# Sinkhorn block attention and token mixer on one core: attention ordered by head pairs, the first batch's V turned on TensorE

## Chip, cores and metric

The kernel runs on one NeuronCore of a Trainium2 chip. The metric is device time in microseconds (us) of one execution: median 109.06 us over three runs of the kernel before (108.4 to 109.84). The profiled execution took 109.01 us, of which the profile's span covers 107.0 us. In what follows a time "at 24.9 us" is counted from the start of that span.

## The reference

```python
for _ in range(5):                                   # sort_net: (4, 8, 8, 8), "Sinkhorn"
    P = np.exp(P - np.max(P, axis=-1, keepdims=True))
    P = P / (np.sum(P, axis=-1, keepdims=True) + 1e-09)
    P = P / (np.sum(P, axis=-2, keepdims=True) + 1e-09)
k_sorted = einsum('bhij,bhjcd->bhicd', P, k_b)       # k, v, q: (4, 8, 768, 64), as 8 blocks of 96
v_sorted = einsum('bhij,bhjcd->bhicd', P, v_b)
scores = scale * q_b @ k_sorted_b^T                  # within each block: 96 x 96
attn = softmax(scores); y = attn @ v_sorted_b
x = y as (4, 768, 512)                               # heads side by side
wq = x @ w_q ; wk = x @ w_k                          # 512 -> 64
mixed = (scale * wq @ wk^T) @ x                      # a token mixer, computed as wq @ (wk^T @ x)
out = relu(mixed) @ w_out                            # (4, 768, 512) fp32
```

## The kernel before

The four batches pass through one pipeline. All inputs are loaded from HBM by DMAs that GpSimd issues, which turn fp32 into bf16: per batch one load of Q, one of K, one of V (786,432 bytes each in SBUF), with three buffers for each of the three, so that the loads of batch 3 reuse the buffers of batch 0. Tokens are laid out so that a partition holds six consecutive tokens (`r` = 0..5) of each head.

The order of the whole program is written out by hand. `ORDER` is a string of items such as `K112`: a letter, a batch, a number and a last character, which for TensorE work is a PSUM bank and for the others an engine (A is ScalarE, D VectorE, P GpSimd, S SyncE). The program walks through it, so each engine gets its instructions in this order and takes them strictly in turn. A capital letter is work on TensorE, and the small letter of the same kind is the copy that takes the result out of PSUM:

- `l`: a load (number 0 is Q, 1 is K, 2 is V, 3 and 4 the weights `wqk` and `wo`). `c`: one of the five Sinkhorn steps (0 subtracts the first maximum), an exponential on ScalarE (L157) and six small VectorE operations. `i`: constants (`idb` the identity, `Lx` a selector, `m_p` a mask, ones and zeros in buffers).
- `U`, `b`, `B`: `U` turns the Sinkhorn result `Pb` on TensorE, `b` copies it to `PbT`, and `B` spreads it over the partitions with eight matmuls by `Lx`. `n`: the product of that with the mask gives `M`, the sorting weights of a batch (L218), for four heads at a time; batch 0 and 1 in parts on VectorE straight from PSUM, the others on GpSimd from the copy `PTR` (`u`).
- `Q`/`q`: 16 transposes each, three per batch, give `QT`. `K`/`k`: 12 matmuls each for a pair of heads (number 0 to 3), sort K and turn it at once, giving `KT`. `V`/`v`: 8 matmuls each, three per batch, give the sorted V in `Vs` with a column of ones beside each head (stride 65).
- `R`: six DMAs per batch on SyncE's queue turn `Vs` (tokens over 128 partitions) into `VT` (96 tokens of a block over 96 partitions).
- `S`/`e`: scores of five (block, head pair) cases each, seven per batch, and their exponential into `E` (L301). `P`, `r`, `x`: weighted sums with 14 (block, head) cases each, five per batch; the ones column yields the softmax's denominator, `r` takes its reciprocal and `x` multiplies (L333), giving `X`.
- `T`/`t`: transposes of `X` into `XT`; `J`/`j`: both 512-to-64 products; `d`, `W`/`w`: moving and turning them; `G`/`g`: wk^T x; `H`/`h`: times wq, with relu, into `mixT`; `O`/`o`: six products with `w_out` of four 512-column matmuls each; `y`: the stores.
- `Z`: matmuls on a buffer of zeros (`fil`) whose result nobody reads. `N`: a one-element GpSimd copy (`gate`) that makes GpSimd wait for an eviction before it goes on to the next loads in its order.

Two details decide when things can start. Scores are numbered by block first (`i, kp = divmod(pr, NP)`, L292), so every group of scores needs the sorted K of all four head pairs. And in `ORDER` K of batch 0 is the fourth load, behind Q and V of batch 0 and K of batch 1; the last three are V of batch 3, K of batch 3 and V of batch 2.

All matmuls are recorded at line 138, all plain copies at L142 (ScalarE) and L144 (VectorE).

Of the kernel before, what the change touches and what calls it, by code (L numbers as in the profile page):

```python
# [18 lines left out]
l00P l02P l11P i00P i03P i02P l01P c00D Z087 c01D i01D c02D l10P Z027 c03D Z027 c04D Q026 Q007 q02A  # L19
c05D Z025 q00A U004 Z026 b00D B007 Z026 n00D u00A Z025 n10P n01D Q014 Z025 q01A V000 n11P Z025 v00D  # L20
K112 K104 k11A V016 k10D R00S Z021 R01S v01A V022 K120 v02D N00v N01v N02v l12P l21P l03P K134 R02S
k12A R03S K036 k13A R04S K010 R05S K022 k03A k01D K004 k02A n20P k00D Z027 l04P Z027 n21P S030 S062
S054 e03A S006 e00A S010 e05A Q127 Q116 e01A q12D S024 q11D Q107 e06A l20P e02A S040 q10D Z026 e04A
Z025 S102 S154 P030 e10A P016 r03D e15A V102 x03D l30P v10A S144 r01D P040 x01D e14A P022 R11S R10S
r04D P006 r02D x04D S114 x02D T031 e11A r00D t03A K202 x00D T020 k20A K234 t02D T011 k23D T007 t01A
V112 J010 t00A S134 v11A j01D S166 J001 d01D e13A W010 R12S V122 j00D R13S w01D e16A n30P W001 v12D
N10v N11v N12v l32P l31P l22P K224 w00A S126 k22A G001 d00D n31P R15S K212 e12A R14S G011 k21D g01A
Q200 H004 q20A H012 Q211 h00D Q227 h01A q21D H024 q22A O010 h02D S252 o01A S206 O051 e25A S214 e20A
o05D S222 O020 e22A P106 e21A O001 r10D x10D o02A P112 P134 o00D S236 Q310 r11D y00S e23A r13D x11D
O031 q31A x13D V326 T103 v32A O040 o03D t10D P144 y01S o04A S246 r14D S262 Q301 x14D e24A y02S Q320  # L30
q30D K314 e26A T137 q32D k31A K322 t13D K300 k32D K334 k30A P126 k33A V312 r12D R34S V300 x12D R35S
v31A S324 v30D e32A S356 R32S T113 R33S T122 e35A t11D S304 R31S S310 t12D R30S J103 e30A V206 e31A
j10D J112 v20D d10S V224 j11A W103 V210 v22A d11S w10D W112 R20S S366 v21D G103 R21S w11A R25S e36A
S334 R24S G113 e33A R23S S340 R22S g11D P346 e34A H122 r34D H114 x34D h12A H100 h11D P326 h10A O143
r32D x32D P224 o14A O122 r22D x22D P200 o12A P216 r20D P242 x20D O135 O114 r21D o13A r24D x21D P230
y11S o11A O105 x24D r23D T214 x23D o10A T207 P312 t21A y10S P305 t20D T231 r31D r30D T220 x31D t23A
J204 O157 t22D j20A x30D J214 o15A T313 d20D j21A y12S T302 t31D W205 d21S W214 t30A P330 w20D G203
w21A r33D J302 x33D G213 j30A T327 g21A W302 d30A T336 t32D w30A H210 t33D H204 H222 h21D G307 h20A
J316 h22A O205 j31D O224 d31A o20D W316 O215 o22D w31A G317 o21A O234 g31A y20S H320 o23A H312 H306
O245 h31A y21S h30D O254 o24A O307 o25A h32D O335 y22S o30D O354 o33D y33S O327 y36S o35A O315 y38S  # L40
o32A O344 y35S o31D y34S o34A y37S
# [4 lines left out]
def kernel(  # L46
# [11 lines left out]
    nc = tc.nc  # L58
# [8 lines left out]
    D1 = D + 1  # L67
    DM = moe_w_out.shape[0]
# [36 lines left out]
    Vs = tiles("Vs", 2, [P, R6, H, D1])  # L105
    VT = tiles("VT", 2, [BLK, NB, H * D1])
    E = tiles("E", 2, [BLK, NT, EW])
    X = tiles("X", 2, [BLK, NB, DM])
# [12 lines left out]
    PbT = sb.tile([NB * NB, BH], BF16, name="PbT")  # L121
    Lx = sb.tile([NB * NB, NB, NB, SP], BF16, name="Lx")
# [4 lines left out]
    fil = sb.tile([P, 512], BF16, name="fil")  # L127

# [21 lines left out]
    def u_c(b, n, e):  # L150
        if n == 0:
            nc.vector.memset(Pm[:, NB:NB + 1, :], 1e-9)
            nc.vector.memset(fil, 0.0)  # L153
            nc.vector.reduce_max(tmp, Pv, axis=AX.X)
            nc.vector.tensor_sub(Pv, Pv, rows(tmp))
            return
        nc.scalar.activation(Pv, Pv, ACT.Exp)  # L157
        nc.vector.reduce_sum(tmp, Pv, axis=AX.X)
        nc.vector.reciprocal(tmp, tmp)
        nc.vector.tensor_mul(Pv, Pv, rows(tmp))  # L160
        nc.vector.reduce_sum(tmp, Pm.rearrange("p i j -> p j i"), axis=AX.X)
        nc.vector.reciprocal(tmp, tmp)
        nc.vector.tensor_mul(Pb if n == 5 else Pv, Pv, cols(tmp))


    def u_i(b, n, e):
        if n == 0:
            nc.gpsimd.memset(idb, 0.0)
            nc.gpsimd.affine_select(out=idb, in_=idb, compare_op=ALU.not_equal, fill=1.0, base=0,
                                    pattern=[[-1, P]], channel_multiplier=1)  # L170
        elif n == 1:
            nc.vector.reduce_max(m_p, idb.rearrange("p (j s) -> p s j", s=SP), axis=AX.X)
        elif n == 3:
            nc.gpsimd.memset(Lx, 0.0)
            nc.gpsimd.affine_select(out=Lx.rearrange("p i j s -> p (i j) s"),
                                    in_=Lx.rearrange("p i j s -> p (i j) s"),
                                    compare_op=ALU.not_equal, fill=1.0, base=0,
                                    pattern=[[-1, NB * NB], [0, SP]], channel_multiplier=1)
        elif n == 2:
            for t in Vs:  # L180
                nc.gpsimd.memset(t[:, :, :, D:D1], 1.0)
            for t in KT:
                nc.gpsimd.memset(t[:, :, S:S + P - BLK], 0.0)
            for t in E:
                nc.gpsimd.memset(t[:, :, 2 * TH * BLK:EW], 0.0)
                nc.gpsimd.memset(t[:, NT - 1, 2 * (NB * NP - TH * (NT - 1)) * BLK:EW], 0.0)
# [12 lines left out]
    def u_U(b, n, bank):  # L199
        mm(bf(bank)[0:NB * NB, 0:BH], Pb.rearrange("p i j -> p (i j)"), idb[0:BH, 0:BH], t=True)  # L200

    def u_b(b, n, e):
        nc.vector.tensor_copy(PbT, bf(U["t"])[0:NB * NB, 0:BH])

    def u_B(b, n, bank):
        for i in range(NB):
            mm(PS[:, bank, i * BH:(i + 1) * BH], Lx[:, i].rearrange("p j s -> p (j s)"), PbT)
# [3 lines left out]
    def u_n(b, n, e):  # L211
        h0, h1 = n * 4, n * 4 + 4
        if b == 0:
            src = PS[:, U["bank"], 0:NB * BH].rearrange("p (i h) -> p h i", h=BH)
        else:
            src = PTR.rearrange("p i h -> p h i")
        src = src[:, b * H + h0:b * H + h1, :]
        ENG[e].tensor_tensor(  # L218
            out=M[b % 2][:, h0:h1], in0=src.unsqueeze(2).to_broadcast([P, 4, SP, NB]),
            in1=m_p.unsqueeze(1).unsqueeze(3).to_broadcast([P, 4, SP, NB]), op=ALU.mult)  # L220
# [5 lines left out]
    def u_Z(b, n, bank):  # L226
        for _ in range(n):
            mm(PS[:, bank, :], fil[:, 0:P], fil)
# [10 lines left out]
    def u_q(b, n, e, bank):  # L239
        copy(e, QT[b % 2][:, :, 2 * n:2 * n + 2, :].rearrange("p k r s -> p k (r s)"),  # L240
             bf(bank).rearrange("p (k s) -> p k s", k=NP))

# [26 lines left out]

    def u_R(b, n, e):  # L270
        ENG[e].dma_start(out=VT[b % 2].rearrange("(s r) i x -> r s i x", r=R6)[n],
                         in_=Vs[b % 2][:, n].rearrange("p h e -> p (h e)"))


    def u_N(b, n, e):
# [7 lines left out]
        elif e == "e":  # L283
            src = t[0:1, n, 0:1]
        else:
            src = t.rearrange("p i m -> p (i m)")[0:1, grp(n)[0] * D:grp(n)[0] * D + 1]
# [3 lines left out]
    def u_S(b, n, bank):  # L290
        for m, pr in enumerate(range(n * TH, min(n * TH + TH, NB * NP))):
            i, kp = divmod(pr, NP)  # L292
# [18 lines left out]
    def u_P(b, n, bank):  # L311
        u0, w = grp(n)
        for m in range(2 * w):
# [3 lines left out]
            mm(PS[:, bank + a, c * D1:(c + 1) * D1], E[b % 2][:, t, x * BLK:x * BLK + P],  # L317
               VT[b % 2][:, u // H, (u % H) * D1:(u % H + 1) * D1])

    def avps(bank, w):  # L320
        return PS[0:BLK, bank:bank + 2, 0:w * D1].rearrange("p a (t e) -> p a t e", e=D1)
# [8 lines left out]
    def u_x(b, n, e, bank):  # L330
        u0, w = grp(n)
        xo = X[b % 2].rearrange("p i m -> p (i m)")[:, u0 * D:(u0 + 2 * w) * D]
# [5 lines left out]
    def u_T(b, n, bank):  # L338
        ps = bf(bank).rearrange("p (t c) -> p t c", t=PT)
        for ii in range(2):  # L340
            for pt in range(PT):
                mm(ps[:, pt, ii * BLK:(ii + 1) * BLK], X[b % 2][:, 2 * n + ii, pt * P:(pt + 1) * P],
                   idb[0:BLK, 0:BLK], t=True)

    def u_t(b, n, e, bank):
        copy(e, XT[b % 2][:, :, 2 * n:2 * n + 2, :].rearrange("p t i c -> p t (i c)"),
             bf(bank).rearrange("p (t c) -> p t c", t=PT)[:, :, 0:2 * BLK])

    def u_J(b, n, bank):
        for pt in range(PT):  # L350
            mm(PS[:, bank, 0:S // 2], wqk[:, pt].rearrange("p a d -> p (a d)"),
               XT[b % 2][:, pt, 4 * n:4 * n + 4, :].rearrange("p i c -> p (i c)"),
# [22 lines left out]
    def u_G(b, n, bank):  # L375
        for i in range(4 * n, 4 * n + 4):
            for a in range(2):
                mm(PS[a * DH:(a + 1) * DH, bank, 0:DM // 2], wk[b % 2][:, i, :],
                   X[b % 2][:, i, a * 256:(a + 1) * 256], start=(i == 0), stop=(i == NB - 1))
# [50 lines left out]
    fills = dict(q="Q", k="K", v="V", e="S", r="P", x="P", t="T", j="J", w="W", g="G", h="H", o="O")  # L430
    for item in ORDER.split():
        kind, b, n, arg = item[0], int(item[1]), int(item[2:-1]), item[-1]
        if kind.isupper() and kind not in "RN":
            banks[kind, b, n] = int(arg)
            if kind in "UB":
                U["t" if kind == "U" else "bank"] = int(arg)
# [36 lines left out]
```

The softmax here doesn't subtract the row's maximum and nothing guards it: scores larger than these inputs give would overflow.

## Time and profile before

| | busy us | share of the 107.0 us |
|---|---|---|
| TensorE matmuls (PE) | 91.9 | 86% |
| VectorE (DVE) | 70.7 | 66% |
| ScalarE (ACT) | 69.8 | 65% |
| GpSimd (POOL) | 27.4 | 26% |
| the queue of the loads | - | 62.7% of 16 DMA engines |
| SyncE's queue (`R`, `y`) | - | 27.5% of 16 DMA engines |

The busy time of a pipelined matmul includes its latency, so it overstates TensorE; of the 91.9 us, 11.9 us are the 30 matmuls on zeros. The text of the prediction reads it from the spacing of matmuls instead.

### The profile page before, as it was taken

The numbers are of one execution on the slowest core, as the hardware profiler recorded it, in microseconds if no ns is written. First come the engines' busy times: TensorE is split into PE (matmuls) and PEld (weight loads), VectorE is DVE, ScalarE is ACT, GpSimd is POOL, SyncE is SP. The second block draws the span as 40 slices with busy tenths as digits, with TensorE's granted clock in tenths as the row PEclk, the third lists the DMA queues.
The fourth block names the chain that finished last, engine by engine and source line by source line (L and its number), as shares of the span: only waits on it lengthen the run. The fifth ranks groups of instructions, "written<-read, shape, count | busy, mean of one in ns | idle before, by whom it ended". The sixth has DMA issues, their size and how long they took to land.

```text
span 107.0 us, 3324 instructions
## 1 busy us (share of the span) xinstructions
PE 91.9 (86%) x1407; PEld 60.9 (57%) x1419; DVE 70.7 (66%) x131; ACT 69.8 (65%) x99; POOL 27.4 (26%) x43
## 2 busy tenths in 40 slices
PE   5917689987798799999999987997999999999930
PEld 2306036774766677755768974864677865534400
DVE  1787550773429968693699994878999768528320
ACT  4104413686999689989689896895266758474420
POOL 6999226049980004880000000000000000000000
PEclk9995555999999999999999999999999999999999
DMA  0899999999999999999999999473045320045981
GB/s 3 91 203 204 203 204 204 204 239 224 222 201 193 202 234 206 213 264 208 204 207 291 291 328 225 95 201 84 6 196 202 130 84 0 6 196 211 383 317 72
DMA packets 19982, 19.94 MB, mean 186 GB/s; under 512 B 1984, under 2 KB 18048, under 8 KB 19968
## 3 DMA queue, kind: packets, MB, share of 16 engines
q0 software_dynamic: 14064, 10.09, 62.7%
q1 hardware_dynamic: 5904, 9.64, 27.5%
q8 instruction: 11, 0.18, 0.6%
q14 instruction: 3, 0.02, 0.1%
HBM read 20.19 MB, written 6.29 MB: 247 GB/s over the span
## 4 chain that ended last, share of the span: by engine, by line
PE 40%; DMA 28%; issue 13%; POOL 10%; DVE 3%; ACT 2%; POOLq 1%; SPq 0%; DVEq 0%
PE ps L138 40%; DMA Vn<-in_v_dram 19%; DMA Qn<-in_q_dram 7%; POOL M L218 3%; DMA VT<-Vs 2%; POOL Vn L100 2%; POOL Qn L100 2%; POOL wqk L192 1%; DVE Vs L144 1%; ACT QT L142 1%; POOL Kn L100 1%; POOLq L468 1%; POOL gate L287 1%; POOL wo L194 1%; ACT ot L142 1%
## 5 line engine op out<-in xcount | busy, mean ns | idle before, releaser
L301 ACT ACTIVATE E<-ps 96x960 bf16<-96x960 f32 (+1 forms) x28 | 23.5, 907 | 3.3 <-PE ps L138 3.1
L138 PE MATMUL ps<-wo,mixT 128*128 128x512 bf16 x88 | 22.2, 380 | 0.5
L333 DVE TENSOR_TENSOR X<-ps,R 96x896 bf16<-96x896 f32 (+1 forms) x20 | 19.7, 999 | 0.4
L142 ACT COPY ot<-ps 128x512 f32<-128x512 f32 x16 | 9.4, 587 | 9.9 <-PE ps L138 8.1
L138 PEld LDWEIGHTS <-mixT 128*128 128x128 bf16 x96 | 8.4, 98 | 9.2 <-issue 0.8
L138 PE MATMUL ps<-fil 128*128 128x512 bf16 x30 | 11.9, 520 | 2.0 <-DVE fil L153 1.2
L218 POOL TENSOR_TENSOR M<-PTR,m_p 128x512 bf16<-128x512 bf16 x6 | 7.9, 1318 | 14.1 <-PE ps L138 10.1
L138 PE MATMUL ps<-VT,E 96*128 96x65 bf16 x256 | 10.7, 194 | 0.9 <-DMA VT<-Vs 0.6
L138 PEld LDWEIGHTS <-E 96*128 96x128 bf16 x256 | 9.6, 98 | 3.2 <-issue 1.7
L138 PE MATMUL ps<-idb,Qn 128*64 128x128 bf16 x192 | 8.1, 244 | 3.6 <-DMA Qn<-in_q_dram 3.0
L138 PEld LDWEIGHTS <-Qn 128*64 128x64 bf16 x192 | 7.0, 125 | 5.5 <-DMA Qn<-in_q_dram 3.5
L138 PE MATMUL ps<-QT,KT 64*128 64x96 bf16 x256 | 9.1, 204 | 1.1 <-ACT E L301 0.8
L144 DVE CAST Vs<-ps 128x1024 bf16<-128x1024 f32 x6 | 7.3, 1224 | 3.9 <-PE ps L138 3.3
L408 DVE TENSOR_SCALAR mixT<-ps 128x1024 bf16<-128x1024 f32 x6 | 7.3, 1218 | 3.7 <-PE ps L138 3.7
L142 ACT CAST KT<-ps 128x768 bf16<-128x768 f32 x10 | 7.6, 806 | 2.5 <-PE ps L138 2.3
L138 PEld LDWEIGHTS <-KT 64*128 64x128 bf16 x256 | 6.2, 94 | 4.5 <-issue 3.6
L138 PE MATMUL ps<-Vn,M 128*128 128x128 bf16 x96 | 7.5, 225 | 0.5 <-DMA Vn<-in_v_dram 0.5
L144 DVE COPY ot<-ps 128x512 f32<-128x512 f32 x8 | 5.4, 685 | 3.6 <-PE ps L138 3.5
L138 PE MATMUL ps<-M,Kn 128*64 128x128 bf16 x192 | 7.1, 221 | 0.8 <-DVE R L328 0.6
L142 ACT COPY QT<-ps 128x1024 bf16<-128x1024 bf16 x6 | 6.0, 1007 | 2.3 <-PE ps L138 2.2
L328 DVE RECIPROCAL R<-ps 96x14 f32<-96x14 f32 (+1 forms) x20 | 4.2, 224 | 5.0 <-PE ps L138 4.9
L138 PEld LDWEIGHTS <-M 128*128 128x128 bf16 x96 | 6.3, 102 | 2.1 <-DMA Vn<-in_v_dram 0.9
(67 smaller groups left out, 130.1 us busy)
## 6 DMA issues: line engine op xcount, KB each, us to landing
out_dram<-ot SPq DMA_DIRECT2D x9, 512.0 KB, 2.7
VT<-Vs SPq DMA_DIRECT2D x24, 130.0 KB, 5.1
Qn<-in_q_dram POOLq DMA_DIRECT2D x4, 768.0 KB, 14.6
Vn<-in_v_dram POOLq DMA_DIRECT2D x4, 768.0 KB, 9.9
Kn<-in_k_dram POOLq DMA_DIRECT2D x4, 768.0 KB, 12.0
out_dram<-ot SPq DMA_DIRECT2D x6, 256.0 KB, 2.1
wo<-in_moe_w_out_dram POOLq DMA_DIRECT2D x1, 512.0 KB, 12.0
qD<-qkT SPq DMA_DIRECT2D x3, 48.0 KB, 2.4
```

The source lines that it names most:

```text
L100: nc.gpsimd.dma_start(out=t[b % NIN].rearrange("p h r d -> p h (r d)"), in_=src[b].rearrange("h (p r) d -> p h (r d)", p=P))
L138: nc.tensor.matmul(o, w, x, is_transpose=t, start=start, stop=stop, skip_group_check=True)
L142: nc.scalar.copy(o, i)
L144: nc.vector.tensor_copy(o, i)
L192: nc.gpsimd.dma_start(out=wqk[:, :, s, :], in_=w.rearrange("(t p) d -> p t d", p=P))
L194: nc.gpsimd.dma_start(out=wo, in_=moe_w_out.rearrange("(t p) d -> p t d", p=P))
L218: ENG[e].tensor_tensor(out=M[b % 2][:, h0:h1], in0=src.unsqueeze(2).to_broadcast([P, 4, SP, NB]), in1=m_p.unsqueeze(1).unsqueeze(3).to_bro ...
L287: nc.gpsimd.tensor_copy(gate, src)
L301: nc.scalar.activation(E[b % 2][:, n, 0:2 * w * BLK].rearrange("p (t a c) -> p a t c", a=2, c=BLK), PS[0:BLK, bank:bank + 2, 0:w * BLK].re ...
L328: nc.vector.reciprocal(rr[b, n][:, :, 0:w], avps(bank, w)[:, :, :, D])
L333: nc.vector.tensor_mul(xo.rearrange("p (a t d) -> p a t d", a=2, d=D), avps(bank, w)[:, :, :, 0:D], rr[b, n][:, :, 0:w].unsqueeze(3).to_br ...
L408: nc.vector.tensor_relu(o, i)
```

## The change

It is one new version of the schedule with several edits, meant to let the attention of batch 0 begin earlier and to free the DMA queues early on.

1. Scores, weighted sums and everything between are ordered by head pair first. `X` is laid out by head pair, each `T` takes one head pair over all eight blocks, and each half of `J` is cut into three matmuls and a last one.
2. V of batch 0 no longer goes through `V`, `v` and `R`. `F` sorts and turns V as `K` does with K, `f` evicts it into a borrowed buffer, `A` turns it back block by block and `a` writes `VT` from PSUM.
3. `U` goes; VectorE transposes `Pb` in 32x32 squares. `Lx` is built by one ScalarE copy of the identity in place of a fill and a select on GpSimd.
4. All Sinkhorn exponentials stand ahead of the q evictions in ScalarE's order. The matmuls on zeros depend on a column that ScalarE writes after each exponential.
5. The mask product of batch 0 is made in four parts of two heads.
6. Heads in `Vs`, `VT` and in the PSUM result of `P` lie 66 apart in place of 65.
7. Loads in a new order: Q, K, V of batch 0, `wqk`, K, Q, V of batch 1, `wo`, Q and K of batch 2, Q of batch 3, V of batches 2 and 3, K of batch 3.

A function for DMA transposes of Q (`D`) is added, but no item uses it.

```diff
@@ ORDER, start and the items around the middle @@
-l00P l02P l11P i00P i03P i02P l01P c00D Z087 c01D i01D c02D l10P Z027 c03D Z027 c04D Q026 Q007 q02A
-c05D Z025 q00A U004 Z026 b00D B007 Z026 n00D u00A Z025 n10P n01D Q014 Z025 q01A V000 n11P Z025 v00D
-K112 K104 k11A V016 k10D R00S Z021 R01S v01A V022 K120 v02D N00v N01v N02v l12P l21P l03P K134 R02S
+l00P l01P l02P i00P i02P l03P c00D c01D i01D Z087 c02D i03A Z257 l11P c03D Z357 c04D Q007 Q016 l10P
+Q025 c05D Z560 q02A q00A b00D B005 Z040 q01A n03D l12P n02D u00A K030 n01D n10P K022 n00D K016 l04P
+k03D K004 k01A n11P k00D S050 S066 e05A k02D F014 e06A f01D F020 F032 f02A S006 f03D S014 l20P e00A
+A021 F002 e01A a02D S036 n21P A010 f00D e03A S044 A031 a01D e04A n20P A007 a03D K112 a00A K104 k11D
...
+t00D V110 R15S t01D e12A V106 J005 n30P v10D v11A N12v N11v l21P N12v N11v N10v l30P l22P S132 l32P
...
+k22A v21D R20S R21S J117 o01A R25S V320 R24S J137 R23S J106 v32D R22S j11A V302 y00S d11A W117 J126
+v30A S204 R35S w11D j10D S230 R34S O027 e20A d10D R31S R30S W106 e23A V312 o02D Q325 w10D y01S v31A
+K320 q32D K306 G104 k32D R32S k30A K332 R33S G114 k33D S300 g11A K316 e30A H124 k31D H112 h12A H100
@@ buffers @@
+    DS = D + 2
-    Vs = tiles("Vs", 2, [P, R6, H, D1])
-    VT = tiles("VT", 2, [BLK, NB, H * D1])
+    Vs = tiles("Vs", 2, [P, R6, H, DS])
+    VT = tiles("VT", 2, [BLK, NB, H * DS])
-    X = tiles("X", 2, [BLK, NB, DM])
+    X = tiles("X", 2, [BLK, NP, NB, P])
@@ u_c @@
         nc.scalar.activation(Pv, Pv, ACT.Exp)
+        nc.scalar.copy(filw[:, n, 0:1], fil[:, 0:1])
@@ u_i @@
-            nc.gpsimd.memset(Lx, 0.0)
-            nc.gpsimd.affine_select(out=Lx.rearrange("p i j s -> p (i j) s"),
-                                    in_=Lx.rearrange("p i j s -> p (i j) s"),
-                                    compare_op=ALU.not_equal, fill=1.0, base=0,
-                                    pattern=[[-1, NB * NB], [0, SP]], channel_multiplier=1)
+            nc.scalar.copy(Lx.rearrange("p i j s -> p (i j) s"),
+                           idb[0:BH, 0:BH].unsqueeze(2).to_broadcast([BH, BH, SP]))
@@ u_U, u_b @@
-        mm(bf(bank)[0:NB * NB, 0:BH], Pb.rearrange("p i j -> p (i j)"), idb[0:BH, 0:BH], t=True)
-        nc.vector.tensor_copy(PbT, bf(U["t"])[0:NB * NB, 0:BH])
+        nc.vector.transpose(PbT.rearrange("p a h -> p (a h)"), Pb.rearrange("p i j -> p (i j)"))
@@ u_n @@
-        h0, h1 = n * 4, n * 4 + 4
+        nh = 2 if b == 0 else 4
+        h0, h1 = n * nh, n * nh + nh
@@ new: V of batch 0 @@
+    def u_F(b, n, bank):
+        ps = flat(bank)
+        for r in range(R6):
+            for hh in range(2):
+                h = 2 * n + hh
+                mm(ps[hh * D:(hh + 1) * D, r * P:(r + 1) * P], Vn[b % NIN][:, h, r, :],
+                   M[b % 2][:, h].rearrange("p s i -> p (s i)"))
+    def u_f(b, n, e, bank):
+        copy(e, ft(b, n).rearrange("p (i s r) -> p i s r", i=NB, s=SP),
+             flat(bank)[:, 0:S].rearrange("p (r s i) -> p i s r", r=R6, s=SP))
+    def u_A(b, n, bank):
+        for i in range(NB):
+            mm(bf(bank)[0:BLK, i * P:(i + 1) * P], ft(b, n)[:, i * BLK:(i + 1) * BLK], idb, t=True)
+    def u_a(b, n, e, bank):
+        copy(e, VT[b % 2].rearrange("p i (h e) -> p i h e", e=DS)[:, :, 2 * n:2 * n + 2, 0:D],
+             bf(bank)[0:BLK].rearrange("p (i h d) -> p i h d", i=NB, h=2))
@@ u_S, u_T, u_J @@
-            i, kp = divmod(pr, NP)
+            kp, i = divmod(pr, NB)
-        for ii in range(2):
-            for pt in range(PT):
-                mm(ps[:, pt, ii * BLK:(ii + 1) * BLK], X[b % 2][:, 2 * n + ii, pt * P:(pt + 1) * P],
-                   idb[0:BLK, 0:BLK], t=True)
+        for i in range(NB):
+            mm(bf(bank)[:, i * BLK:(i + 1) * BLK], X[b % 2][:, n, i, :], idb[0:BLK, 0:BLK], t=True)
-        for pt in range(PT):
+        m = n % 2
+        for pt in range(PT - 1) if n < 2 else (PT - 1,):
```

## Prediction

> **What bounds the kernel now.** I read the page's forty slices first, then the chain that ended last, then the timeline of TensorE, then busy time by stage.
>
> ```profile
> PE   5917689987798799999999987997999999999930
> DVE  1787550773429968693699994878999768528320
> ACT  4104413686999689989689896895266758474420
> PEclk9995555999999999999999999999999999999999
> DMA  0899999999999999999999999473045320045981
> ```
>
> A slice is 2.68 us. The DMA row is full from slice 2 to slice 25, until about 66 us: the loads fill the DMA engines for the first 60% of the run. PE is nearly full from slice 10 (27 us) to 103 us. Before that it is busy only by name: many of its matmuls are on zeros.
>
> ```profile
> 45.56 20.11 DMA Vn<-in_v_dram
> 65.68 0.05 issue
> 65.72 4.94 PE ps L138 x84
> ...
> 102.66 0.02 issue
> 102.68 0.58 ACT ot L142
> ```
>
> In the chain the last load (V of batch 2) lands at 65.7 us, and from there PE runs through to 102.6 us, 36.9 us later. Then come a copy, the last store and the end of the span (4.4 us), and 2.0 us lie between the span and the reported time.
>
> ```profile
> 23.96 1.02 PE L138 MATMUL ps<-fil 128*128 128x512 bf16 x3 [0.18 <-ACT KT L142]
> 24.91 1.01 PE L138 MATMUL ps<-QT,KT 64*128 64x96 bf16 x34
> 26.47 0.39 PE L138 MATMUL ps<-QT,KT 64*128 64x96 bf16 x10 [0.55 <-ACT E L301]
> ```
>
> In PE's timeline scores begin only at 24.9 us, though Q of batch 0 landed at 8.6 us. From there ACT's exponentials set the pace.
>
> ```profile
> 24.00:36.00 12.00, 10.16 (x238) 7.85 (x239) 6.85 (x13) 10.12 (x13) 7.56 (x9) 1.00 1.35 210
> 36.00:66.00 30.00, 28.18 (x554) 20.86 (x554) 23.55 (x37) 26.93 (x35) 5.80 (x8) 1.00 1.23 243
> 66.00:82.00 16.00, 15.09 (x250) 10.96 (x250) 13.58 (x23) 9.92 (x15) 0.00 (x0) 1.00 0.44 132
> ```
>
> By stage (columns: length, busy PE, weight loads, DVE, ACT, POOL, clock, DMA, GB/s) DVE has 6.85 of 12 us in the first stage and then 23.6 of 30. So three things bind together: loads until 66 us, PE's total, and evictions that lend PE its banks.
>
> **What the Trainium skill says.** "DMA: Bandwidth & Descriptors", section "Issuing engines are not separate DMA queues": DMAs of all issuers share the same 16 engines and interleave. The trace agrees: with loads alone 203-205 GB/s move, and while the turns `R` of batch 0 run, every load in the queue lands later (K of batch 0 at 20.2 us, the next load at 25.5). "TensorE: Matmul & The Clock Gate", Part 1: an idle window returns the array to half clock. Here PE idles for 3.0 us before 8.7 us and the clock row shows 5 until about 18 us. "VectorE: DVE Perf Modes", "The three transpose paths": VectorE transposes in 32x32 squares only, straight into SBUF; nothing in this trace shows one.
>
> **Unit prices.** From the spacing of matmuls in PE's timeline: K group of 12, 0.44 us (12 within 0.46; 36 in 1.2); V of 8, 0.50; S of 10, 0.28; P of 14, 0.47; T of 8, 0.41; Q of 16, 0.56; O of 4, 0.86. J, W, G and H of a batch together take 3.5. Summed over the order, PE needs 77 us before. ACT's and DVE's groups have the page's means: exponential 0.975, K eviction 0.81 or 0.96, V eviction 1.03 or 1.23, Q eviction 1.01 or 0.69, X product 1.08 plus reciprocal 0.23.
>
> **The change by parts.**
>
> *Start.* The fifth exponential waits only 0.06 us for a q copy, so moving it brings that. Step 2's last VectorE operation took 0.87 us against 0.21, ending with GpSimd's select for `Lx`: without that select -0.65. The small copies after the exponentials, and `Lx` on ACT (0.5, estimated from its 512 elements beside the 384-element copies), lie in ACT's idle gaps: nothing. `Pb` thus ends at 11.8 in place of 12.5. `U` and `b` took 0.48 up to `PbT`. One VectorE transpose on 32x64 I put at 0.2, like the other operations on that shape; bounds 0.1 and 0.4. Before, `B` also stood behind two fills until 13.66; after, it runs at 12.0. A half-sized mask product is about 0.37 (0.69 before), so the first K group starts at 13.2 and all four products end at 14.2. Fills are 28 against 30, but 14 of the old ones ran after 14.4 us and none of the new do.
>
> *First scores.* Loads land 3.86 us apart (786,432 bytes at 204 GB/s): Q 8.6, K 12.5, V 16.4 us. Scores of head pair 3 need Q's three copies (ACT, until 13.4) and one K eviction (DVE 14.2 to 15.2). So they start at 15.4 us, 9.5 us earlier.
>
> *V of batch 0.* F is 4 K groups (1.76), A is 4 groups of 8 transposes (1.64), less three V groups: PE +1.9 us. Evictions: one f and one a on ACT (0.81 + 1.01), three each on DVE (3 x 0.96 + 3 x 0.69), together 6.8 us against 3.5. This lies in the stretch from 16 to 24 us that PE and DVE before spent largely waiting. Six turns of 130 KB go. In 22-28 us of the trace 244, 235 and 223 GB/s move in place of 204; over 20-28 us the 6 turns beside 1.0 MB of loads cost about 3.1 us of DMA.
>
> *Until 33 us.* ACT is the tightest: from 15.7 us e0 (6.3), f, a, the first K and Q evictions of batch 1 and its first V copies follow each other for 17.3 us. At 33 us my sums put the queues at PE 18.5, ACT 21, DVE 19.5 us of work done. At the same time before: PE 14, ACT 17, DVE 9.5. The remaining work is 60.7 (79.2 in all) against 64.8 on PE and 47 against 56 on DVE. Lead on PE 4.1 us, already net of F and A.
>
> *Loads.* GpSimd's order puts K of batch 2 behind a mask product and gates on batch 1's V evictions. V of batch 1 lands at 28.7 and its copies end near 34, so that load is issued at about 35. Behind that wait stand four more loads and one mask product. Queued before it are `wo` and Q of batch 2, which last until about 36 us with the turns of batch 1 among them: a bubble of 0 to 1 us. Up to the last load the DMA moves the same loads, twelve to eighteen turns in place of eighteen (0.5 us each) and two stores of 512 KB in place of three (about 1.5 us at 340 GB/s). So K of batch 3 lands at 65.7 - 1.5 - (0 to 3.1) + (0 to 1): 61 to 65, middle 63.
>
> *After the last load.* PE's work in the order from the first K group of batch 3 is 35.4 us. From the first V group of batch 2 it was 35.3 before. With the same 1.6 us of losses the end comes 36.9 us after the landing: 63 + 36.9 = 99.9. By the lead alone it would be 102.6 - 4.1 = 98.5. PE would get to that K group at about 61 us if nothing held it, so it waits about 2 us, while evictions catch up. I take 99.2, between the two: 99.2 + 4.4 + 2.0 = **105.6 us**.
>
> *At nothing.* T, J, G and the X layout keep their counts and sizes. A stride of 66 makes a turn 1.5% larger (0.05 us a batch) and leaves P's 65 columns; whether the even stride speeds a read no row shows, so 0, with up to -0.5 in the range.
>
> **Rivals.** (1) *The lead is given back at the loads*: the bubble is 2 us or more (GpSimd reaches its gates late) and all turns still fall before the last load, so it lands near 65.5 and the end stays: 109. For it: before, PE waited for that load too. Against: six turns fewer. (2) *The whole lead and fewer losses*: DVE has 9 us less left and from 33 us PE loses half of the 6 us it lost before: 98.5 - 3 + 6.4 = 102. For it: DVE's load in the middle stages. Against: ACT has almost as much left (54.6 against 55.4). (3) *Slower*: the last load is now K, with the whole chain of its batch behind it: K evictions, 6.3 us of exponentials, X products, then the mixer. If it lands at 65 and half of those exponentials plus the K evictions (3.2 + 1.8) lie bare on PE, 65 + 36.9 + 5.0 + 6.4 = 113.3. For it: ACT and DVE have some 16 us each beside PE's 17.6 in that stage. Against: P, O and T of batches 1 and 2 stand between as filler.
>
> **Numbers.** The forecast 0.50, rival 1 0.20, rival 2 0.18, rival 3 0.12. Faster by 2% means under 106.9: all of rival 2 and most of the forecast's spread (0.42 of 0.50), 0.60. Within 2%: the rest of the forecast and most of rival 1, 0.27; slower 0.13. For 8 in 10 the range reaches from rival 2's value to just past rival 1's, 102.0 to 109.4.
>
> **What would show it.** Right: a first score matmul at 15 to 17 us; no clock of 5 between 9 and 18 us; no turn before 29 us; DMA full until 61 to 65 us; PE's end at 97 to 101. Wrong: scores after 19 us; a hole in the DMA row at 35-38 us; PE idle for more than 3 us at K of batch 3; or ACT as PE's main releaser after 60 us.

## The result and the profile after

The changed kernel takes 104.91 us (four runs, 104.28 to 105.69) beside 108.83 us: a ratio of 0.963, 95% interval 0.9535 to 0.9726. The forecast was 105.6. A later repeat of five rounds gave 0.9634 (0.9584 to 0.9684). Ratios below are always to the kernel before, run beside each experiment on the same chip; they leave out executions that ran longer at a lower granted clock, and since no_warm and before_no_q3 were profiled in such an execution, only the start is read of the first trace and nothing of the second.

The changed kernel's page, part 2 (forty slices of 2.55 us):

```profile
PE   3987897999988996968989998999999999999940
DVE  3877689889994957359997777878889987046200
ACT  5231948998869999539898797979995669556650
PEclk9999999999999999999999999999999999999998
DMA  0899999999999989999999999960630500055992
GB/s 3 86 205 203 203 204 187 202 210 198 204 208 204 239 118 216 237 206 203 205 204 203 253 335 315 337 214 0 278 140 0 225 6 0 19 206 206 370 344 109
```

The clock row has no more 5. DVE is at 8 or 9 tenths from slice 6 to slice 11 (15 to 31 us), where slices 6 to 11 of the old page read 0, 7, 7, 3, 4 and 2. The DMA row is still full to 66 us, with one dent: slice 14, about 36 to 38 us, moves 118 GB/s. The prediction had listed a hole at 35 to 38 us among the signs of being wrong, while its own sum allowed a bubble of up to 1 us there.

The chain of work that ended last, in the changed kernel (start, length, what):

```profile
10.40 19.28 DMA Vn<-in_v_dram
...
38.99 1.24 POOL M L220
40.23 21.48 DMA Kn<-in_k_dram
61.70 0.04 issue
61.75 0.59 PE ps L140 x15
62.34 3.39 DMA VT<-Vs
65.73 32.34 PE ps L140 x398
```

The last load, now K of batch 3, lands at 61.7 us, 4.0 us before the last load of the old kernel. TensorE ends at 98.06 us, 4.6 us before its old end.

TensorE's timeline after, where the scores begin:

```profile
13.37 1.80 PE L140 MATMUL ps<-M,Kn 128*64 128x128 bf16 x48
15.51 0.47 PE L140 MATMUL ps<-QT,KT 64*128 64x96 bf16 x14 [0.34 <-DVE KT L146]
16.37 1.44 PE L140 MATMUL ps<-M,Vn 128*64 128x128 bf16 x36 [0.39 <-DVE KT L146]
```

Scores start at 15.51 us where it was 24.91. The third row is `F`: Vn as weights, M moving.

Where the time came from shows in busy time by stage (length, then busy PE, weight loads, DVE, ACT, POOL; clock; DMA; GB/s). Before:

```profile
15.00:25.00 10.00, 9.50 (x149) 6.38 (x148) 5.92 (x6) 6.01 (x8) 4.96 (x8) 0.84 1.29 217
25.00:36.00 11.00, 9.21 (x235) 7.51 (x236) 5.85 (x12) 9.51 (x12) 6.56 (x7) 1.00 1.37 206
```

After:

```profile
15.00:25.00 10.00, 9.01 (x226) 7.48 (x221) 9.18 (x14) 8.93 (x12) 5.80 (x6) 1.00 1.41 199
25.00:36.00 11.00, 10.21 (x212) 7.75 (x212) 9.21 (x16) 9.75 (x12) 2.90 (x6) 1.00 1.25 213
```

PE's busy time alone would say that nothing happened from 15 to 25 us: 9.5 against 9.0. The counts say more: 149 matmuls, of which 11 on zeros are busy for 3.85 us, against 226 with none on zeros. DVE and ACT together went from 12 us of work to 18. The lead of 9.4 us at the first scores shrinks on the way: 6.3 us at the first product with `w_out` (47.05 to 40.74), 4.6 at the end. By the prices of the prediction, summed over `ORDER`, PE has 75.2 us of work left at the first scores after the change and 70.0 before (estimates), since K of batch 1 and V now come later and `F` and `A` are extra. 9.4 - 5.2 leaves 4.2; the remaining 0.4 would be less waiting, which is not shown.

### The profile page after: what moved, and what is told of

It reads as the page before. It is cut to its first block, busy times and chain, and to the rows that moved or that the text cites. A ratio compares the mean times of both kernels' runs of the same rounds, so it can differ in the third digit from the quotient of the medians.

```text
span 101.9 us, 3431 instructions
## 1 busy us (share of the span) xinstructions
PE 90.3 (89%) x1468; PEld 60.4 (59%) x1468; DVE 71.8 (71%) x137; ACT 73.8 (72%) x108; POOL 24.9 (24%) x42
## 4 chain that ended last, share of the span: by engine, by line
DMA 43%; PE 35%; POOL 15%; issue 2%; POOLq 1%; ACT 1%
PE ps L140 35%; DMA Kn<-in_k_dram 21%; DMA Vn<-in_v_dram 19%; DMA VT<-Vs 3%; POOL Kn L101 3%; POOL Qn L101 3%; POOL M L220 2%; POOL Vn L101 2%; POOL wqk L195 1%; POOL E L189 1%; POOL gate L322 1%; POOLq L502 1%; ACT ot L144 1%; POOL E L188 0%; POOL VT L182 0%
## 5 line engine op out<-in xcount | busy, mean ns | idle before, releaser
L144 ACT COPY ot<-ps 128x512 f32<-128x512 f32 x20 | 11.6, 586 | 5.2 <-PE ps L140 4.6
L140 PE MATMUL ps<-fil,filw 128*128 128x512 bf16 x28 | 8.6, 455 | 2.4 <-DVE filw L156 1.6
L144 ACT CAST KT<-ps 128x768 bf16<-128x768 f32 x8 | 6.3, 798 | 5.0 <-PE ps L140 4.9
L146 DVE CAST KT<-ps 128x768 bf16<-128x768 f32 x8 | 7.5, 954 | 2.0 <-PE ps L140 1.7
L140 PE MATMUL ps<-idb,X 96*128 96x96 bf16 x128 | 7.5, 206 | 0.3 <-issue 0.3
L140 PEld LDWEIGHTS <-Kn 128*64 128x64 bf16 x192 | 5.9, 109 | 3.1 <-DMA Kn<-in_k_dram 2.0
L140 PEld LDWEIGHTS <-X 96*128 96x128 bf16 x128 | 6.0, 98 | 2.0 <-issue 0.9
L140 PE MATMUL ps<-idb,Qn 128*64 128x128 bf16 x192 | 6.6, 220 | 0.7 <-DMA Qn<-in_q_dram 0.7
L440 ACT ACTIVATE mixT<-ps 128x1024 bf16<-128x1024 f32 x7 | 6.8, 1022 | 0.3 <-PE ps L140 0.2
L140 PE MATMUL ps<-XT,wqk 128*128 128x384 bf16 x32 | 6.9, 327 | 0.0
```

The costliest lines, as they stand in the source:

```text
L140: nc.tensor.matmul(o, w, x, is_transpose=t, start=start, stop=stop, skip_group_check=True)
L144: nc.scalar.copy(o, i)
L146: nc.vector.tensor_copy(o, i)
L440: nc.scalar.activation(o, i, ACT.Relu)
```

## Experiments

Each is a small edit of the changed kernel, unless said otherwise; `...` marks where a line of `ORDER` is cut short. The order by head pairs and the order of the loads (parts 1 and 7 of the change) were never undone alone, so the gain is not split among all the parts.

**Yardstick.** 

> The changed kernel itself, unchanged, as the yardstick for the runs beside it. Every theory expects 104.3 to 105.7 us, the last load landing near 61.7 us and TensorE ending 36.3 us later.

Measured: 105.28 us, ratio 0.9634; the last load at 62.5, TensorE's end 36.4 us later.

**The stride of 66.**

```diff
-    DS = D + 2
+    DS = D + 1
```

> One part undone: V heads 65 apart in place of 66. Theory A (no row of either trace gets faster through the stride: the weighted sums have 194 ns a matmul before and 193 after, V evictions 1.02 and 1.22 us in both) expects the changed kernel's time within 0.3 us. Rival: if unaligned reads cost TensorE or the turns something that the mean hides, 0.5 us or more slower.

Measured: 104.80 us, ratio 0.9605 (0.9566 to 0.9644). The stride brings nothing that can be seen.

**V of batch 0 by DMA turns again.**

```diff
-... F014 e06A f01D F020 F032 f02A S006 f03D S014 l20P e00A A021 F002 e01A a02D S036 n21P A010 f00D
-e03A S044 A031 a01D e04A n20P A007 a03D K112 a00A K104 k11D
+... V004 e06A v00D R00S R01S V010 V022 v01A R02S R03S S006 v02D R04S R05S S014 l20P e00A
+e01A S036 n21P e03A S044 e04A n20P K112 K104 k11D
```

> One part undone: V of batch 0 goes through the V groups and six turns by DMA again; the 48 + 32 matmuls and eight evictions of the other way are left out. Theory A (the loads end earlier because six turns fewer run, and batch 0's weighted sums need no turn): the turns add 2.5 to 3.1 us of DMA ahead of the last load, which lands at 63.5 to 65; batch 0's sums start about 3 us later than at 22.7 us; the time goes up by 1.5 to 3 us, to 106.5 to 108. Rival C (the engines' work alone counts): TensorE does 1.9 us less and the evictions fall by 3.3 us, so it is equal or up to 1 us faster.

Measured: 113.65 us, ratio 1.0417 (1.0367 to 1.0468): 8.4 us slower than the changed kernel and slower than the kernel before. Both theories missed it. TensorE's timeline of this run:

```profile
21.97 1.49 PE L140 MATMUL ps<-M,Kn 128*64 128x128 bf16 x24 [1.11 <-DMA Kn<-in_k_dram]
30.13 1.37 PE L140 MATMUL ps<-VT,E 96*128 96x65 bf16 x22 [6.67 <-DMA VT<-Vs]
31.43 0.85 PE L140 MATMUL ps<-M,Kn 128*64 128x128 bf16 x12
```

and its busy time by stage:

```profile
24.00:30.00 6.00, 0.00 (x0) 0.00 (x0) 0.00 (x0) 0.30 (x1) 0.00 (x0) 0.50 1.25 239
30.00:36.00 6.00, 5.87 (x115) 5.30 (x116) 4.15 (x7) 2.74 (x4) 0.00 (x0) 0.58 1.28 205
36.00:46.00 10.00, 9.73 (x201) 7.60 (x199) 7.40 (x14) 9.38 (x13) 4.47 (x9) 1.00 0.48 80
```

The first turn is issued at 18.55 us. The last is handed to the DMA queue at 21.85 us and lands 8.1 us later, at 30.0, among the queued loads. No packet of a turn moves before 22.5 us, 4 us after the first issue, and why is not shown; from 23 to 28 us the turns move about 0.14 MB per us and the loads 0.11 beside them, where the loads alone moved 0.20. Batch 0's weighted sums stand next in order on TensorE, so it waits 6.67 us and they start at 30.13 us (22.73 in the changed kernel). With it all engines stop, and the clock is at half until 34 us. GpSimd then comes to the gates ahead of K of batch 2 only at 42.4 us (34.2 in the changed kernel), and the DMA engines move 80 GB/s from 36 to 46 us.

**Is it the bare wait or the dry loads?** The same with K of batch 2 loaded early (see the next edit but one).

> V of batch 0 by turns again, and K of batch 2 loaded early (both edits of the two runs before). In the run with turns alone TensorE stood 6.7 us at batch 0's first weighted sums, waiting for the last of six turns, and the loads then ran dry for some 8 us, because they stand behind gates on batch 1's V evictions. Theory A1 (the bare wait is the loss; the dry loads are only its echo, since TensorE comes to everything later too): 110.5 to 112.5 us, some 8 us above the changed kernel with K early (103.2), TensorE's wait still 6 to 7 us. Rival A2 (the dry loads are the loss): 105 to 107.

Measured: 111.98 us, ratio 1.0273 (1.0196 to 1.0351), with a wait of 7.25 us at the same place. That is 8.8 us above the kernel with K early alone. The dry loads are not the loss, so A2 falls, and the number is the one that A1 gave. The next run tests whether the wait itself is the loss.

**The same with the order refitted.** V by turns and K of batch 2 early, as in the run before; K, Q and one group of scores go ahead of batch 0's weighted sums.

```diff
-... K112 K104 k11D P040 k10A P006 r04D K132 x04D P034 r00D k13A S020 x00D e02A K122 r03D Q127 x03D k12A
-Q116 P020 q11A q12D T035 Q104 r02D t03A x02D P012 q10A r01D T025 x01D V120 ...
+... K112 K104 k11D k10A K132 k13A S020 e02A K122 k12A Q127 q12D Q116 q11A Q104 q10A P040 r04D P006 x04D
+P034 r00D x00D r03D x03D P020 T035 r02D t03A x02D P012 r01D T025 x01D V120 ...
```

> As the run beside it, with the order refitted to the turns: K, Q and scores of batch 0 that do not need VT are put ahead of batch 0's weighted sums, as the kernel before does with other work. Theory A1: the turns land at 30 us as before, TensorE meanwhile does 4 us of other work, its wait falls to 2 to 4 us, and the time to 105.5 to 108: so the TensorE way of turning V is worth 2 to 5 us rather than 8. Rival C (only engine work counts): 102 to 103.5, as F and A are gone.

Measured: 111.79 us, ratio 1.0213 (1.0129 to 1.0297): a miss. Its TensorE timeline:

```profile
28.22 2.77 PE L140 MATMUL ps<-idb,Qn 128*64 128x128 bf16 x48 [1.70 <-DMA Qn<-in_q_dram]
30.92 2.30 PE L140 MATMUL ps<-VT,E 96*128 96x65 bf16 x50
35.18 0.82 PE L140 MATMUL ps<-idb,X 96*128 96x96 bf16 x8 [1.96 <-DVE X L370]
```

The wait for VT is gone, but TensorE waits for Q instead and then for X, since the five X products come one after the other from 31.9 us on. The clock row (slices of 2.75 us) is low as well:

```profile
PEclk9999999855578558999999999999999999999999
```

From 22 to 30 us and from 36 to 41 us half the clock was granted, so part of the loss is slower matmuls; how much was not separated from the waiting. The time is still 8.6 us above the kernel with K early alone. So the 8 us are not the stall of one instruction, and A1 in its bare form falls too. As I read it, batch 0 cannot go on without V, and until batch 1 has landed there is too little else. Whether another order hides the turns for less in this layout was not tried. The kernel before does at 109, by sorting K of two batches and V of one before any scores.

**K of batch 2 early.** Its buffer has been free from the start, and its place behind the gates is only an order of GpSimd.

```diff
-... l20P e00A
+... l20P l21P e00A
-... N12v N11v l21P N12v N11v N10v l30P ...
+... N12v N11v N12v N11v N10v l30P ...
```

> The load of K of batch 2, whose buffer has been free from the start, is issued right behind Q of batch 2 in place of after the gates on batch 1's V evictions. Theory A: the hole in the DMA row at 36 to 38 us (97 GB/s, about 1.1 us of transfer) closes, TensorE's 0.8 us wait for that load at 44.35 us goes, the last load lands about 1 us earlier, and the time falls by 0.3 to 1.0 us, to about 104.2. Rival B (the end follows the last load one for one): falls by 1.0 us or more. Rival: the queue is fuller when batch 1's turns run, they land later and batch 1's weighted sums wait, no gain or up to 0.5 us slower.

Measured: 103.21 us, ratio 0.9451 (0.9412 to 0.9490), 2.1 us below the yardstick and the best version found. The yardstick by stage, at the dent:

```profile
36.00:38.00 2.00, 0.00 (x0) 0.00 (x0) 0.00 (x0) 1.00 0.64 88
```

With K early:

```profile
36.00:38.00 2.00, 0.00 (x0) 0.00 (x0) 0.00 (x0) 1.00 1.24 239
```

(The rows count only instructions on the tile `Kn`; read the last two columns, the DMA share and GB/s.) TensorE's timeline of the yardstick at the two loads:

```profile
44.51 1.20 PE L140 MATMUL ps<-M,Kn 128*64 128x128 bf16 x36 [0.65 <-DMA Kn<-in_k_dram]
...
62.55 0.86 PE L140 MATMUL ps<-M,Kn 128*64 128x128 bf16 x24 [0.94 <-DMA Kn<-in_k_dram]
```

and with K early:

```profile
43.49 1.20 PE L140 MATMUL ps<-M,Kn 128*64 128x128 bf16 x36
...
60.33 0.84 PE L140 MATMUL ps<-M,Kn 128*64 128x128 bf16 x24
```

The waits of 0.65 and 0.94 us are gone, and the end comes 1.8 us earlier in the profiles. That is more than theory A gave it: it had counted the first wait and not the second. The number lies in the range of rival B, too (the end follows the last load one for one). TensorE uses the last load at 60.33 us without waiting, so it landed at least 2.2 us earlier, and this run alone does not tell A from B.

**A load less, with K early.** Q of batch 3 is not loaded, its work uses the buffer's old content.

```diff
-... l30P l22P ...
+... l22P ...
```

> The changed kernel with K of batch 2 early, and the load of Q of batch 3 left out as in the run beside it. TensorE no longer waited for the last load in the kernel with K early, so theory A (engines set its end) expects 102.7 to 103.4, no more than 0.5 us below 103.2, though the last load lands 3.9 us earlier. Rival B (loads still set the end): 101.5 or less.

Measured: 102.62 us, ratio 0.9424 (0.9397 to 0.9451), some 0.3 us below the ratio with K early, with overlapping intervals. B would have it at 101.5 or less: once the dent is closed, the loads no longer set the end.

**The same load less, in the kernel before.**

```diff
-... x03D l30P v10A ...
+... x03D v10A ...
```

> The kernel before with one load less: Q of batch 3 is not loaded and its work runs on the Q of batch 0 still in that buffer. Theory A (the last load sets the end before the change): V of batch 2 lands about 3.9 us earlier than 65.7; TensorE comes to it only some 0.5 us earlier than it does now, since it waited 0.5 us there, so the end moves by 0.5 to 1.5 us: 107.5 to 108.5. Rival B (the end follows the last load one for one): 105 to 105.5. Rival C (the load did not matter): 108.6 to 109.

Measured: ratio 0.9968 (0.9942 to 0.9994), 108.5 us by that ratio: 0.35 us less, at the edge between A and C. The end did not come 3.9 us earlier, as B has it. That the last load itself landed earlier is not shown, so B is unlikely for the old kernel rather than refuted.

**A later start, with K early.**

```diff
-... Z040 ...
+... Z0140 ...
```

> The changed kernel with K of batch 2 early and ten more matmuls on zeros ahead of the first K group, which makes it start 2.1 us later, at 15.5 us. Theory A (TensorE and the evictions behind it set the end, but it waits 0.6 us for Q and 0.6 us for V of batch 1): 0.8 to 1.8 us of the 2.1 reach the end, 104.0 to 105.0. Rival (the start has slack, as in the kernel before, where 1.6 us of head start brought nothing): 103.0 to 103.5.

Measured: 103.56 us, ratio 0.9511 (0.9484 to 0.9538), 0.65 us above the ratio with K early, the intervals touching: less than expected. Its timeline at V of batch 1:

```profile
15.59 1.53 PE L140 MATMUL ps<-M,Kn 128*64 128x128 bf16 x48
...
30.68 0.61 PE L140 MATMUL ps<-Vn,M 128*128 128x128 bf16 x8
```

K starts 2.2 us later, but V of batch 1 only 0.8 (29.89 with K early): by then waits for loads have taken most of it up.

**Two start parts undone.**

```diff
-Q025 c05D Z560 q02A q00A b00D B005 Z040 q01A n03D l12P n02D u00A K030 n01D n10P K022 n00D K016 ...
+Q025 q00A c05D Z560 q02A b00D B005 Z040 q01A n01D l12P u00A K030 n00D n10P K022 K016 ...
-        nh = 2 if b == 0 else 4
+        nh = 4
```

> Two parts undone together: one q eviction stands ahead of the fifth exponential again, and the mask product of batch 0 is made in two parts of four heads. Theory A: the exponential starts about 0.3 us later (10.3 in place of 10.04 us) and the first K group 0.6 us later (14.0 in place of 13.37); the scores of batch 0 start 0.3 to 0.7 us later, but TensorE waits 0.3 us for V of batch 1 at 29.7 us all the same, so at most 0.4 us reaches the end: 105.0 to 105.7 beside 105.2. Rival (a head start is kept to the end): 0.6 us or more slower.

Measured: 104.95 us, ratio 0.9617 (0.9564 to 0.9670). The exponentials ahead of all q evictions and the mask in quarters bring nothing that can be measured. The first K group starts at 13.59 us, 0.2 later than with them, not 0.6.

**The new start in the kernel before.** The `Lx` copy, the VectorE transpose, the order of the exponential and the mask quarters, put into the old kernel; its start of `ORDER` becomes:

```diff
-l00P l02P l11P i00P i03P i02P l01P c00D Z087 c01D i01D c02D l10P Z027 c03D Z027 c04D Q026 Q007 q02A
-c05D Z025 q00A U004 Z026 b00D B007 Z026 n00D u00A Z025 n10P n01D ...
+l00P l02P l11P i00P i02P l01P c00D Z087 c01D i01D c02D i03A l10P Z027 c03D Z027 c04D Q026 Q007
+c05D q02A Z025 q00A Z026 b00D B007 Z026 n00D n01D u00A Z025 n10P n02D n03D ...
```

> The kernel before with the new start alone: Lx by a ScalarE copy, Pb transposed on VectorE, the fifth exponential ahead of the q evictions, the mask in four parts; its loads, its order and its V path stay. Theory A: M comes about 1 us earlier (13 in place of 14.2 us), but K of batch 0 lands only at 20.2 us, so the first scores stay at 24.9 us within 0.4 and the time within 0.5 us of the kernel before (109.2). Rival: the start alone brings 1 us or more.

Measured: ratio 1.0017 (0.9989 to 1.0045). Its TensorE timeline:

```profile
20.88 1.53 PE L138 MATMUL ps<-M,Kn 128*64 128x128 bf16 x48 [1.30 <-DMA Kn<-in_k_dram]
...
26.74 1.08 PE L138 MATMUL ps<-idb,Qn 128*64 128x128 bf16 x32 [1.22 <-DMA Qn<-in_q_dram]
```

Against my expectation the scores did start earlier, at 23.31 us in place of 24.91, but TensorE then waits 1.2 us for Q of batch 1. No load had been brought forward for this start, and it was given back at the next load.

**Without the warming matmuls.**

```diff
-... c02D i03A Z257 l11P c03D Z357 c04D ...
+... c02D i03A l11P c03D c04D ...
```

> The changed kernel without the ten matmuls on zeros that wait for the second and third exponential. TensorE idles from about 5 to 8.6 us. Theory A (they keep the granted clock up): the clock row shows 5 from about 8 us until 12 to 18 us as it did before the change, Q's transposes take 2.5 to 3 in place of 1.5 us, the first K groups longer, scores start up to 0.5 us later, the end 0 to 0.5 us later. Rival: no drop of the clock, since other fills follow; no change at all.

Measured: ratio 0.9692 (0.9638 to 0.9747), about 0.6 us over the yardstick's ratio, the intervals overlapping. The start of its TensorE timeline:

```profile
1.64 3.60 PE L140 MATMUL ps<-fil,filw 128*128 128x512 bf16 x8 [1.64 <-DVE filw L156]
8.68 2.77 PE L140 MATMUL ps<-idb,Qn 128*64 128x128 bf16 x48 [3.44 <-DMA Qn<-in_q_dram]
11.78 2.13 PE L140 MATMUL ps<-fil,filw 128*128 128x512 bf16 x5 [0.33 <-issue]
...
15.11 1.81 PE L140 MATMUL ps<-M,Kn 128*64 128x128 bf16 x48
```

and of the changed kernel:

```profile
6.88 1.25 PE L140 MATMUL ps<-fil,filw 128*128 128x512 bf16 x5 [0.44 <-ACT filw L161]
8.63 1.53 PE L140 MATMUL ps<-idb,Qn 128*64 128x128 bf16 x48 [0.50 <-DMA Qn<-in_q_dram]
```

The 48 transposes take 2.77 us in place of 1.53, five matmuls on zeros 2.13 in place of 1.25, and the first K group starts 1.7 us later, more than I had put. The clock row, though, reads 9 over this whole stretch, not 5 as theory A expects. So the run shows slower matmuls and not the granted clock behind them; the 2.77 us are what the same transposes took in v0_dma_fit at a clock of 0.50.

## Why the prediction was right

*Start, first scores.* Right to a few tenths: `Pb` done at 11.8 (11.8), the VectorE transpose 0.23 us (0.2), `B` at 12.11 (12.0), first K at 13.37 (13.2), scores at 15.51 (15.4), the foretold time in brackets. (The prediction's count of 30 matmuls on zeros before is that of the trace's records; the program has 34.) But start_old, k2_late2 and before_start show that tenths of a microsecond there are worth little: 2.2 us of delay cost about 0.65. What made the start pay, as v0_dma suggests, is that batch 0 could run through while batch 1 was still loading.

*V of batch 0.* The terms were +1.9 us of PE, 3.3 us more of evictions, and 3.1 us of DMA saved. The right mechanism was in the text only as the lead; no term priced what the old way would cost in the new order. That is 8.4 us in this order. In the trace it begins with the turns' landing at 30.0 us, which a price by bytes (the 3.1 us) does not give.

*Until 33 us.* The lead of 4.1 us net is near what came out, 4.6 at the end, but partly by luck: with K early TensorE ends at 97.1 us, a lead of 5.6, which suggests that the lead was put too low and that some of it was given back at the dent. (The 14 us of PE work put down as done before do not fit: 77 less the 64.8 left is 12.2, which is also what the trace's matmuls come to at the same prices. The lead rests on the 64.8.) V of batch 1 landed at 29.7, not 28.7.

*Loads.* K of batch 2 was issued at 34.6 (35), the bubble was there (97 GB/s from 36 to 38 us, so 2 x (204 - 97) / 204 = 1.0 us lost; foretold 0 to 1), the last load landed at 61.7 (61 to 65, middle 63). The statement of the Trainium skill ("DMA: Bandwidth & Descriptors", "Issuing engines are not separate DMA queues") that all issuers' DMAs share the engines held: in v0_dma the turns and the loads moved 0.14 and 0.11 MB per us side by side, and the six turns of batch 0 landed a median of 7.0 us after issue.

*After the last load.* 36.4 us from landing to TensorE's end (36.9). As a rule it seems right by balance, not by cause: taking a load away moved the old kernel by 0.35 us and the kernel with K early by 0.3. TensorE waited 0.28 us there (0.94 in the repeat), not 2. "I take 99.2, between the two" therefore leaned somewhat too far towards the loads; the lead alone gave 98.5, the traces show 98.06 and, in the repeat, 98.9. From TensorE's end to the end of the span it was 3.8 us (4.4), and from the span to the reported time 2.4 (2.0).

*Rivals.* The first (the lead given back at the loads) happened in small: the bubble cost 1.0 us of transfer, and closing it brought 2.1 us, so about that much had been given back. The third did not: after 60 us TensorE's only waits of note are 0.3 us (0.9 in the repeat) for K of batch 3, and none is for ACT. The second, 102, was not reached; the kernel with K early, which is a further change, comes to 103.2.

## What to carry to other kernels

Price a DMA round trip inside the chip by when it lands under the queue's load and by what stands behind it on the engine that needs it, not by its bytes; 80 matmuls in place of 24 and 1.9 us more of TensorE were the cheaper way here, while loads filled the queue. When loads pace a pipeline, look for those that wait in an issue order without needing to: moving one item brought 2.1 us on top of the whole change's 3.9. A head start is worth only as much as the next load lets through, so shift work and its loads together.

## What the runs showed of the hardware

- In v0_dma, a turn of 132 KB within SBUF landed up to 8.1 us after issue while loads were queued, and 2.3 us at the least elsewhere in that run.
- TensorE's transposes went with the granted clock: 48 took 1.53 us in the changed kernel at a clock of 1.00, and 2.77 us in v0_dma_fit at 0.50.
- In the kernel before, a VectorE operation on two SBUF tensors took 0.87 us where it takes 0.21, and ended with GpSimd's select; with the select gone all five took 0.21 to 0.33. The Trainium skill ("SBUF — State Buffer", section "SBUF: two separate sides") describes the port pair that VectorE and GpSimd share as an exclusive lock held for a whole instruction, so that the one that comes second blocks; a VectorE operation with two SBUF inputs needs it only against a GpSimd operation that reads SBUF, as the select does. The trace agrees for this operation: it began at 6.28 us, inside the select (5.61 to 7.11 us), and ended at 7.15. The one of 0.33 us in the changed kernel began at 4.34 us, inside the select that builds `idb` (4.31 to 4.60).
